# Attention in a fixed order: the four PSUM score banks as one tile, and as two tiles of one step each

## The chip, the core and the metric

The kernel runs on one NeuronCore of one Trainium2 chip, as one program. Its time is the device time of that core in microseconds, and the number that counts is the median of several executions. The inputs and the output lie in the chip's memory; the host only rearranges the inputs before the start.

## The reference

Three stages follow each other. The change is in the first.

```python
def _attn_ref(q, k, v):                      # (4, 8, 576, 64) each
    scores = scale * np.matmul(q, k.transpose(0, 1, 3, 2))
    rel = pos[:, None] - pos[None, :]
    bias = slopes[:, None, None] * (-np.abs(rel))[None]
    mask = (rel >= 0) & (rel < 128)
    scores = np.where(mask, scores + bias[None], -1e9)
    attn = np.exp(scores - scores.max(-1, keepdims=True))
    attn = attn / (attn.sum(-1, keepdims=True) + 1e-9)
    return np.matmul(attn, v)

def _moe_ref(x, phi, w1, w2):                # x: (2304, 512), 8 experts, 4 slots each
    logits = x @ phi
    d = softmax of logits over the tokens;  c = softmax over the slots
    slots = d.T @ x
    slot_out[e] = np.maximum(slots[e] @ w1[e], 0) @ w2[e]
    return c @ slot_out

def _moe2_ref(x, w_in, w_out):               # d_ff = 2048
    h = x @ w_in
    return (h * np.clip(h + 3, 0, 6) / 6) @ w_out
```

All data are 32-bit floats. A row of the scores has at most 128 valid keys, since the window is 128.

## The kernel before

**The steps.** There are four batches `b`. In a batch the 576 tokens are cut into five tiles `i` of 128 rows (the last has 64), and the eight heads into four couples `j`. One (b, i, j) is a step, 80 in all, and two steps that follow each other are a pair: 40 pairs, two for each tile. Below, pair "1a" is the first pair of a tile with i = 1, pair "1b" its second.

**One step.** `emit_s` (L179 to L212) does four small matmuls on TensorE (L190), one for each head (`u`) and half of the 64 rows (`hf`). Their output is `sp[64e..., m, hf, c0:c1]`, where `m` is the step's place in its pair (0 or 1) and `hf` picks the half. The tile `sp` (L148) is 128 x 2 x 2 x 512 floats, so that each (m, hf) fills a PSUM bank of its own: two banks for the first step of a pair, two for the second. VectorE then reads each half out of PSUM (L202): it scales it, adds the bias and keeps the smallest value of each row. ScalarE takes the exponent and the row sums (L210). After both steps of a pair VectorE makes the reciprocals (`emit_norm`, L217 and L219) and GpSimd multiplies (L224). Two steps later TensorE transposes the result (`emit_t`, L237) and VectorE or ScalarE copies it out (L239). Four steps later TensorE multiplies it with V (`emit_pv`, L257).

**Side work.** For every finished tile there are smaller steps: `side_x` (transposes L274, copy L277), `side_l` (L283, L285), and, for groups of tiles, `side_max` (L296, L298 to L321), `side_e` (L328, L335, L336) and `side_s` (L345, L351). Those that write PSUM share one buffer, the tag `m`.

**What sets the order.** It is written by hand. Inside `manual_schedule` (L477) each engine gets its instructions as the Python code issues them, in the sequence of L30 for each pair: `s0 s1 p0 p1 b0 t0 n0 t1 x0`, that is both steps' scores, two products with V of the pair before last, one piece of side work, two transposes with the norm between them, another piece of side work. No engine takes a later instruction ahead of an earlier one that waits. The semaphores are not written by hand: they follow from which tile an instruction writes and which it reads.

**Transfers.** SP's queue issues them in the order of `do_s` (L434): at the first pair of tile m, q of tile m+1, k and v of tile m+2 (256 KB each), then one expert weight (1 MB). From tile 17 on it issues weights until no buffer is free. A transfer whose buffer is still being read holds back all that stand behind it on that queue.

**Other users of the score banks.** `last_l` (L359) and `last_max` (L391) at the end of attention, and the matmuls at L506 that keep TensorE busy before the next stage, borrow parts of `sp`.

Of the kernel before, what the change touches and what calls it, by code (L numbers as in the profile page):

```python
# [9 lines left out]
F32 = mybir.dt.float32  # L10
# [34 lines left out]
def nq(i):  # L45
    return 128 if i < 4 else 64
# [3 lines left out]
def body(ctx: ExitStack, tc, q, k, v, phi, we, wf, cst, sel, out):  # L50
    nc = tc.nc
# [3 lines left out]
    ident, blk, dup = conp[:, 0:128], conp[:, 128:256], conp[:, 256:384]  # L55
# [73 lines left out]
    with ExitStack() as a:  # L129
# [9 lines left out]
        ps_s = a.enter_context(tc.tile_pool(name="ps_s", bufs=1, space=PSUM))  # L139
# [5 lines left out]
        bias8 = cona.rearrange("p (j h c) -> p j h c", j=NP, h=2)  # L145
        xb = [tp.tile([128, 2, 2, 128], F32, name=f"xb{n}") for n in range(2)]
        pb = [tp.tile([128, 448], F32, name=f"pb{n}") for n in range(NPB)]
        sp = ps_s.tile([128, 2, 2, 512], F32, name="sp")  # L148
        acc = cp.tile([128, 128], F32, name="acc")
        el = cp.tile([128, S], F32, name="el")  # L150
        vt = {}
# [27 lines left out]
        def emit_s(n):  # L179
            b, i, j = steps[n]  # L180
            hs = halves(i)
            w, m = nq(i), n % 2
            for e in range(2):
                for u in range(2):
                    hf = u ^ e
                    if hf >= len(hs):
                        continue
                    c0, c1 = hs[hf][1:]
                    g = 2 * (i - 1) + hf
                    nc.tensor.matmul(  # L190
                        out=sp[64 * e:64 * e + 64, m, hf, c0:c1],
                        lhsT=qz[64 * u:64 * u + 64, (NB * b + i) % 2,
                                j * w + 64 * hf:j * w + 64 * hf + 64],
                        rhs=kt[64 * u:64 * u + 64, g + c0 // 64:g + 3, j],
                        start=True, stop=True)
            p = pb[n % NPB]
            P[n] = p
            if not m:
                ST[0] = sm.tile([128, 3, 4], F32, tag="st", name=f"st{n}")
            st = ST[0]  # L200
            for hf, c0, c1 in hs:
                nc.vector.tensor_tensor_reduce(  # L202
                    out=p[:, 256 * hf + c0:256 * hf + c1],
                    in0=sp[:, m, hf, c0:c1], in1=bias8[:, j, hf, c0:c1],
                    scale=-0.125, scalar=3.0e38, op0=ALU.add, op1=ALU.min,
                    accum_out=st[:, 0, 2 * m + hf:2 * m + hf + 1])
            for hf, c0, c1 in hs:
                x = p[:, 256 * hf + c0:256 * hf + c1]
                r = slice(2 * m + hf, 2 * m + hf + 1)
                nc.scalar.activation(out=x, in_=x, func=AF.Exp, bias=st[:, 0, r], scale=-1.0,  # L210
                                     accum_out=st[:, 1, r])
            return p, st, hs  # L212
# [74 lines left out]
        run = {}  # L287
# [66 lines left out]
        def last_l(i):  # L354
            c0, w = 128 * (i - 3), nq(i)
            if i == 3:
                run["lg"] = sp[:, 0, 0, 0:192]
            for j in range(NP):
                nc.tensor.matmul(out=run["lg"][:, c0:c0 + w],  # L359
                                 lhsT=phi4[:, j].rearrange("p g s -> p (g s)"),  # L360
                                 rhs=xt[B - 1, i][:, j, 0:w], start=j == 0, stop=j == NP - 1)

        def last_max():
            mx = ep.tile([128, 8], F32, tag="mx", name="mxl")
            lg, nm, al, z, fz = run["lg"], mx[:, 2:3], mx[:, 6:7], mx[:, 4:5], mx[:, 5:6]
            nc.vector.reduce_max(out=mx[:, 0:1], in_=lg, axis=AX.X)
            nc.vector.scalar_tensor_tensor(out=nm, in0=mx[:, 0:1], scalar=-1.0, in1=run["nm"],
                                           op0=ALU.mult, op1=ALU.min)
            nc.scalar.copy(out=el[0:32, 0:192], in_=lg[0:32])
            nc.scalar.activation(out=el[:, 256:448], in_=lg, func=AF.Exp, bias=nm, accum_out=z)  # L370
            nc.scalar.activation(out=al, in_=run["nm"], func=AF.Exp, bias=nm, scale=-1.0)
            t = ps_m.tile([128, 2, 2, NS], F32, tag="m", name="lnl")
            for r in (1, 0):
                for i in range(2):
                    o = 256 * r + 128 * i
                    nc.tensor.transpose(out=t[0:nq(3 + i), i, r], in_=el[0:32, o:o + nq(3 + i)],
                                        identity=ident[0:32, 0:32])
            e = ep.tile([128, NB, NS], F32, tag="e", name="el2", bufs=1)
            nc.scalar.copy(out=e[:, 0], in_=t[:, 0, 1])
            nc.scalar.copy(out=e[0:64, 1], in_=t[0:64, 1, 1])  # L380
            nc.vector.scalar_tensor_tensor(out=z, in0=run["z"], scalar=al, in1=z,
                                           op0=ALU.mult, op1=ALU.add)
            nc.vector.tensor_scalar(out=fz, in0=z, scalar1=EPS, scalar2=None, op0=ALU.add)
            nc.vector.reciprocal(out=fz, in_=fz)
            nc.vector.tensor_scalar(out=acc, in0=acc, scalar1=al, scalar2=fz, op0=ALU.mult,
                                    op1=ALU.mult)
            t2 = sp[:, 0, 1, 0:128]
            for i in range(2):
                w = nq(3 + i)
                for g in range(4):  # L390
                    nc.tensor.matmul(out=t2[32 * g:32 * g + 32, :], lhsT=e[0:w, i],  # L391
                                     rhs=xn[B - 1, 3 + i][0:w, 128 * g:128 * g + 128],
                                     start=i == 0, stop=i == 1)
            nc.vector.scalar_tensor_tensor(out=acc, in0=t2, scalar=fz, in1=acc, op0=ALU.mult,
                                           op1=ALU.add)
            o = NB * (B - 1) + 3
            nc.scalar.copy(out=cn[:, o], in_=t[:, 0, 0])
            nc.scalar.copy(out=cn[0:64, o + 1], in_=t[0:64, 1, 0])
# [102 lines left out]
        for c in range(2):  # L501
            nc.vector.tensor_copy(
                out=sT2[:, 2 * c:2 * c + 2],
                in_=t[:, 2 * c:2 * c + 2].to_broadcast([128, 2, 2, NS]))
        for _ in range(WARM_A):
            nc.tensor.matmul(out=sp[:, 1, 0, 0:128], lhsT=ident, rhs=ident, start=True, stop=True)  # L506
    pools["z"] = xctx.enter_context(tc.tile_pool(name="zpool", bufs=1, side="left",
                                                 reuse_waits="tile"))
    free["z"] = 1
# [96 lines left out]
    with ExitStack() as bx:  # L606
# [4 lines left out]
        with tc.manual_schedule():  # L611
# [7 lines left out]
                                    in1=rm[:, 0].unsqueeze(2).to_broadcast(wide),  # L619
# [7 lines left out]
                                    in1=rm[:, 1].unsqueeze(2).to_broadcast(wide),  # L627
# [99 lines left out]
            for n in range(16):  # L727
                G, fc = n // 8, n % 8
                w = take(16 + n)
                for g in range(4):  # L730
                    nc.tensor.matmul(out=so[32 * g:32 * g + 8, :], lhsT=hz[:, fc, G, g, :],
                                     rhs=w[g], start=n == 0, stop=n == 15)
# [17 lines left out]
            for G in range(2):  # L750
                L["last"] = nc.vector.tensor_copy(
                    out=L["soT"][:, :, 16 * G:16 * G + 16].rearrange("p c (g j) -> p c g j", g=4),
# [308 lines left out]
```

## Time and profile before

| | us |
|---|---|
| three runs | 416.51, 417.2, 419.62 (median 417.2) |
| the profiled execution's own time | 420.83 |
| its span, first to last instruction | 419.0 |
| score matmuls L190: first and last start | 6.1, 201.0 |
| TensorE busy | 354.7 (85% of the span) |
| VectorE, ScalarE, GpSimd busy | 195.5, 184.7, 81.7 |
| mean granted TensorE clock, share of full speed | 0.918 |

The profile shows one execution. Busy shares are means over stages with quite different limits, so a wait has to be read in its stage: attention fills the span from about 6 to 212 us. On an engine with a fixed order a wait delays all that follows it on that engine. A matmul's end is modelled, so where two groups of matmuls follow each other the distance of their starts says more than their lengths. The granted clock is 1.00 or 0.50 in any short stretch, which is 2.4 or 1.2 GHz.

### The profile page before, as it was taken

To read this page: it belongs to the slowest core of one execution; us is meant where nothing else is said; L and a number is where in the kernel's file an instruction comes from. 1 tells how busy PE (TensorE), PEld (TensorE's weight loads), DVE (VectorE), ACT (ScalarE), POOL (GpSimd) and SP (SyncE) were. 2 spreads that over 40 slices of the span, in tenths; PEclk is the share of its full clock that TensorE was granted. 3 is DMA by queue.
4 is the path that set the end of the run, shared out by engine and by line. 5 is a ranking of instruction groups with operands and counts; after the bars stand their busy time and mean duration, and the time that the engine had idled before them with its cause. 6 is when DMAs were issued, how large, how long until landed. Compare 5 with 4: busy or idle time off the path is not lost. (4 is left out here: it accounts for less than half of the span.)

```text
span 419.0 us, 7556 instructions
## 1 busy us (share of the span) xinstructions
PE 354.7 (85%) x2738; PEld 211.1 (50%) x2738; DVE 195.5 (47%) x617; ACT 184.7 (44%) x551; POOL 81.7 (20%) x182
## 2 busy tenths in 40 slices
PE   6887877778778878786879995599999999999995
PEld 5455544454445544554553321343333436878883
DVE  1454445544354434453242108488888737871000
ACT  3566566656576665563421133522222205642210
POOL 2334223333234223331100220000000001210000
PEclk9599999989699995997959999569999999999999
DMA  8406574445714467091586999886200000112112
GB/s 276 128 21 217 196 261 163 153 175 177 302 40 152 178 230 274 13 360 70 200 296 251 424 383 418 364 276 225 101 0 2 1 1 19 59 75 77 75 75 82
DMA packets 19835, 71.10 MB, mean 170 GB/s; under 512 B 2672, under 2 KB 4848, under 8 KB 13776
## 3 DMA queue, kind: packets, MB, share of 16 engines
q1 hardware_dynamic: 18576, 69.08, 44.6%
q10 hardware_dynamic: 1216, 1.47, 1.0%
q8 instruction: 23, 0.38, 0.4%
q14 instruction: 20, 0.16, 0.1%
HBM read 65.83 MB, written 4.72 MB: 168 GB/s over the span
## 5 line engine op out<-in xcount | busy, mean ns | idle before, releaser
L224 POOL TENSOR_TENSOR pb<-pb,st 128x192 f32<-128x192 f32 (+2 forms) x144 | 63.3, 470 | 140.1 <-DVE st L219 65.4
L210 ACT ACTIVATE pb<-pb,st 128x192 f32<-128x192 f32 (+2 forms) x144 | 61.9, 430 | 46.0 <-DVE st L202 46.0
L190 PE MATMUL sp<-kt,qz 64*64 64x192 f32 (+2 forms) x576 | 46.9, 361 | 34.5 <-DVE st L202 32.5
L202 DVE CUSTOM_DVE_ANT_0 pb<-sp,cona 128x192 f32<-128x192 f32 (+2 forms) x144 | 43.3, 333 | 60.9 <-PE sp L190 50.8
L805 PE MATMUL q<-F,mf 128*128 128x512 f32 x128 | 63.3, 628 | 3.8 <-DVE mf L793 3.8
L190 PEld LDWEIGHTS sp<-kt,qz 64*64 64x64 f32 x576 | 17.7, 143 | 57.2 <-DVE st L202 47.3
L257 PE MATMUL o<-xb,v 128*64 128x128 f32 (+2 forms) x576 | 44.3, 289 | 0.1
L838 PE MATMUL acc<-qhi,P 128*128 128x512 f32 x140 | 42.1, 395 | 0.0
L237 PE MATMUL t<-conp,pb 128*128 128x128 f32 x256 | 41.4, 306 | 0.0
L805 PEld LDWEIGHTS q<-F,mf 128*128 128x128 f32 x128 | 23.3, 197 | 33.4 <-issue 22.6
L257 PEld LDWEIGHTS o<-xb,v 128*64 128x64 f32 (+1 forms) x576 | 32.8, 145 | 13.4 <-issue 11.3
L237 PEld LDWEIGHTS t<-conp,pb 128*128 128x128 f32 x256 | 32.1, 157 | 5.4 <-issue 3.3
L838 PEld LDWEIGHTS acc<-qhi,P 128*128 128x128 f32 x140 | 25.9, 188 | 6.1
L239 ACT COPY xb<-t 128x512 f32<-128x512 f32 (+1 forms) x40 | 19.7, 493 | 19.6 <-PE t L237 19.5
L239 DVE COPY xb<-t 128x512 f32<-128x512 f32 (+1 forms) x40 | 23.2, 580 | 10.8 <-PE t L237 10.2
L210 ACT ACTIVATION_READ_ACCUMULATOR pb<-pb,st 128x1 f32 x144 | 26.9, 187 | 0.0
L853 ACT ACTIVATE out<-acc 128x512 f32<-128x512 f32 (+1 forms) x18 | 10.5, 585 | 30.9 <-PE acc L838 23.3
L838 PE MATMUL acc<-qlo,P 128*128 128x512 f32 x56 | 22.1, 395 | 0.0
L795 POOL COPY mf<-mt 128x64 f32<-128x64 f32 x8 | 5.9, 735 | 80.2 <-ACT mt L785 53.7
L777 ACT COPY m<-mp 128x256 f32<-128x256 f32 x8 | 3.0, 372 | 42.0 <-PE mp L774 42.0
L274 PE MATMUL xps<-conp,xt 128*128 128x128 f32 (+1 forms) x76 | 13.1, 298 | 9.0 <-ACT el L314 8.5
L585 DVE TENSOR_TENSOR pf<-R,As 128x512 f32<-128x512 f32 (+1 forms) x20 | 12.7, 637 | 14.1 <-ACT As L569 7.8
(153 smaller groups left out, 454.6 us busy)
## 6 DMA issues: line engine op xcount, KB each, us to landing
w<-in_we_dram SPq DMA_DIRECT2D x30, 1024.0 KB, 6.3
w<-in_wf_dram SPq DMA_DIRECT2D x16, 1024.0 KB, 8.1
out_dram<-out SPq DMA_DIRECT2D x17, 256.0 KB, 2.0
v<-in_v_dram SPq DMA_DIRECT2D x16, 256.0 KB, 2.8
qz<-in_q_dram SPq DMA_DIRECT2D x15, 256.0 KB, 5.0
kt<-in_k_dram SPq DMA_DIRECT2D x15, 256.0 KB, 5.5
kt<-in_we_dram SPq DMA_DIRECT2D x1, 1024.0 KB, 7.3
qz<-in_q_dram SPq DMA_DIRECT2D x6, 128.0 KB, 5.2
```

The costliest lines, as they stand in the source:

```text
L190: nc.tensor.matmul(out=sp[64 * e:64 * e + 64, m, hf, c0:c1], lhsT=qz[64 * u:64 * u + 64, (NB * b + i) % 2, j * w + 64 * hf:j * w + 64 * hf ...
L202: nc.vector.tensor_tensor_reduce(out=p[:, 256 * hf + c0:256 * hf + c1], in0=sp[:, m, hf, c0:c1], in1=bias8[:, j, hf, c0:c1], scale=-0.125, ...
L210: nc.scalar.activation(out=x, in_=x, func=AF.Exp, bias=st[:, 0, r], scale=-1.0, accum_out=st[:, 1, r])
L224: nc.gpsimd.tensor_tensor(out=x, in0=x, in1=st[:, 2, 2 * m + hf:2 * m + hf + 1].to_broadcast([128, c1 - c0]), op=ALU.mult)
L237: nc.tensor.transpose(out=t[:, c, hf], in_=p[:, o:o + 128], identity=ident)
L239: f(out=x[:, p0:2, 0:nh], in_=t[:, p0:2, 0:nh])
L257: nc.tensor.matmul(out=o[64 * u:64 * u + 64, j, 0:w], lhsT=vv[0:kk, 128 * j + 64 * u:128 * j + 64 * u + 64], rhs=y, start=m == 0, stop=m = ...
L274: nc.tensor.transpose(out=t[0:w, j, :], in_=xt[b, i][:, j, 0:w], identity=ident)
L585: nc.vector.tensor_tensor(out=pf, in0=t[:, 0:w], in1=(L["a2"][s % 2] if j == 4 else A[s])[:, 0:w], op=ALU.mult)
L805: nc.tensor.matmul(out=Q[pt], lhsT=mm[p][:, u, 128 * pt:128 * pt + 128], rhs=F[:, u], start=p == u == 0, stop=p == 7 and u == 1)
L838: nc.tensor.matmul(out=acc, lhsT=l, rhs=r[:, j], start=j == 0 and i == 0, stop=j == 4 and i == 1)
L853: nc.scalar.activation(out=o[:, cs], in_=acc[:, cs], func=AF.Copy, scale=1.0 / 6.0))
```

## The change

The one tile `sp` of four banks becomes a list of two tiles with two banks each, `sp[0]` for the first step of a pair and `sp[1]` for the second. Shapes, sizes and the number of banks in use stay as they were.

```diff
-        sp = ps_s.tile([128, 2, 2, 512], F32, name="sp")
+        sp = [ps_s.tile([128, 2, 512], F32, name=f"sp{n}") for n in range(2)]
...
-                        out=sp[64 * e:64 * e + 64, m, hf, c0:c1],
+                        out=sp[m][64 * e:64 * e + 64, hf, c0:c1],
...
-                    in0=sp[:, m, hf, c0:c1], in1=bias8[:, j, hf, c0:c1],
+                    in0=sp[m][:, hf, c0:c1], in1=bias8[:, j, hf, c0:c1],
...
-                run["lg"] = sp[:, 0, 0, 0:192]
+                run["lg"] = sp[0][:, 0, 0:192]
...
-            t2 = sp[:, 0, 1, 0:128]
+            t2 = sp[1][:, 1, 0:128]
...
-            nc.tensor.matmul(out=sp[:, 1, 0, 0:128], lhsT=ident, rhs=ident, start=True, stop=True)
+            nc.tensor.matmul(out=sp[1][:, 0, 0:128], lhsT=ident, rhs=ident, start=True, stop=True)
```

No engine gets an instruction more, fewer or in another place. What differs is which event an instruction waits for. On TensorE, the first pair of the program (pair 0a of the first batch, L190), before; the name in brackets is the semaphore, here VectorE's:

```order
L190 MATMUL sp<-kt,qz 64x64 [waits DMAHW2_49,DMAHW1_49]
L190 MATMUL sp<-kt,qz 64x128 x2
L190 MATMUL sp<-kt,qz 64x64
L190 MATMUL sp<-kt,qz 64x64 [waits DVE_49]
L190 MATMUL sp<-kt,qz 64x128 x2
L190 MATMUL sp<-kt,qz 64x64
```

and with the change, where 116 and 117 are the two new tiles:

```order
L190 MATMUL sp_116<-kt,qz 64x64 [waits DMAHW2_49,DMAHW1_49]
L190 MATMUL sp_116<-kt,qz 64x128 x2
L190 MATMUL sp_116<-kt,qz 64x64
L190 MATMUL sp_117<-kt,qz 64x64
L190 MATMUL sp_117<-kt,qz 64x128 x2
L190 MATMUL sp_117<-kt,qz 64x64
```

The second step's matmuls had waited for VectorE's two readings (L202) of the first step, which lie in other banks; that wait is gone. In later pairs both programs show a wait on VectorE at both steps, but for other readings. The second pair of the second tile on TensorE, before:

```order
L190 MATMUL sp<-kt,qz 64x192 [waits DVE_49]
L190 MATMUL sp<-kt,qz 64x192 x3
L190 MATMUL sp<-kt,qz 64x192 [waits DVE_49]
L190 MATMUL sp<-kt,qz 64x192 x3
L257 MATMUL o_0_233<-xb_110,v_0_140 64x128 x2
```

and the same pair with the change:

```order
L190 MATMUL sp_116<-kt,qz 64x192 [waits DVE_49]
L190 MATMUL sp_116<-kt,qz 64x192 x3
L190 MATMUL sp_117<-kt,qz 64x192 [waits DVE_49]
L190 MATMUL sp_117<-kt,qz 64x192 x3
L257 MATMUL o_0_234<-xb_110,v_0_141 64x128 [waits DVE_49]
L257 MATMUL o_0_234<-xb_110,v_0_141 64x128
```

Each step now waits for the readings of the step in the same place of the pair before; in the program before, the second step waited for those of the first step of its own pair. The product with V (L257) shows a wait for VectorE's copy L239 of the pair before, which the earlier wait at L190 used to include. There are 60 such places at L190, 38 at L257 and one at L359; VectorE, ScalarE, GpSimd and SP wait for what they waited for.

## Rows read from the trace of the kernel before

**Rows 1.** The page: span, and busy time of the first two engines and the others

```profile
span 419.0 us, 7556 instructions
...
PE 354.7 (85%) x2738; PEld 211.1 (50%) x2738; DVE 195.5 (47%) x617; ACT 184.7 (44%) x551; POOL 81.7 (20%) x182
```

**Rows 2.** Waits of PE up to 204 us: total us, times, longest

```profile
PE sp L190 <- DVE st L202: 32.5, 41, 1.1
```

**Rows 3.** Timeline of PE, pairs 3b and 4a: start, length, instruction, idle before

```profile
133.73 0.56 PE L190 MATMUL sp<-kt,qz 64*64 64x192 f32 x8
135.16 0.56 PE L190 MATMUL sp<-kt,qz 64*64 64x192 f32 x8 [0.88 <-DVE st L202]
135.65 1.09 PE L257 MATMUL o<-xb,v 128*64 128x128 f32 x16
...
139.72 0.54 PE L190 MATMUL sp<-kt,qz 64*64 64x192 f32 x4
140.84 0.54 PE L190 MATMUL sp<-kt,qz 64*64 64x192 f32 x4 [0.58 <-DVE st L202]
141.31 1.09 PE L257 MATMUL o<-xb,v 128*64 128x128 f32 x16
```

**Rows 4.** Timeline of PE, pair 0b

```profile
53.85 0.44 PE L190 MATMUL sp<-kt,qz 64*64 64x64 f32 x8
54.97 0.44 PE L190 MATMUL sp<-kt,qz 64*64 64x64 f32 x8 [0.67 <-DVE st L202]
55.34 1.12 PE L257 MATMUL o<-xb,v 128*64 128x64 f32 x16
```

**Rows 5.** Timeline of all engines, pairs 1a and 1b

```profile
60.99 0.44 ACT L210 ACTIVATE pb<-pb,st 128x192 f32<-128x192 f32 x1
...
61.97 0.46 ACT L210 ACTIVATE pb<-pb,st 128x192 f32<-128x192 f32 x1 [0.45 <-DVE st L202]
...
62.87 0.19 ACT L335 COPY e<-ln 128x64 f32<-128x64 f32 x1
...
63.09 0.22 DVE L336 COPY cn<-ln 128x64 f32<-128x64 f32 x1 [0.87 <-ACT e L335]
...
63.37 0.32 PE L283 MATMUL lps<-xt,phi 128*32 128x64 f32 x8 [0.53 <-DVE cn L336]
...
67.07 0.56 ACT L268 COPY xt<-o 128x512 f32<-128x512 f32 x1
...
67.69 0.66 PE L274 MATMUL xps<-conp,xt 128*128 128x128 f32 x4
```

**Rows 6.** Timeline of SP's queue, tiles 17 and 18

```profile
178.18 2.35 SPq L114 DMA_DIRECT2D w<-in_we_dram  x4
180.57 0.44 SPq L161 DMA_DIRECT2D qz<-in_q_dram  x1
```

**Rows 7.** Timeline of PE, pair 4a of the last batch

```profile
192.53 0.54 PE L190 MATMUL sp<-kt,qz 64*64 64x192 f32 x4 [2.01 <-issue]
```

**Rows 8.** Windows, whole pairs: stretch, us, busy time of engines, clock, DMA share, GB/s

```profile
59.41:68.27 8.86, 6.58 (x91) 4.08 (x90) 5.00 (x27) 5.96 (x22) 3.16 (x8) 1.00 0.89 340
108.45:118.99 10.54, 8.79 (x92) 5.11 (x91) 4.89 (x26) 6.08 (x22) 3.15 (x8) 0.70 0.68 261
157.40:169.71 12.31, 10.34 (x91) 6.62 (x90) 5.34 (x27) 6.16 (x22) 3.37 (x9) 0.58 0.62 234
139.72:143.98 4.26, 3.68 (x44) 2.45 (x43) 2.31 (x10) 2.11 (x8) 1.90 (x4) 1.00 0.75 298
89.01:94.83 5.82, 5.24 (x44) 3.73 (x43) 2.55 (x11) 2.11 (x8) 1.90 (x4) 0.71 0.46 184
```

**Rows 9.** Windows just before the clock fell to 0.50, same columns

```profile
87.50:90.90 3.40, 1.93 (x19) 1.11 (x20) 1.51 (x7) 2.63 (x8) 1.02 (x3) 1.00 1.01 393
104.60:108.00 3.40, 2.08 (x21) 1.54 (x20) 0.98 (x7) 2.37 (x10) 0.00 (x0) 1.00 0.60 177
155.80:159.20 3.40, 1.48 (x20) 0.78 (x20) 1.45 (x8) 2.62 (x9) 1.17 (x4) 1.00 1.02 390
```

## The prediction

> **What bounds the kernel now.** I read the page's busy times first: TensorE is busy 354.7 of 419.0 us, every other engine less than half [rows 1]. A share of 85% is a mean over stages, so next come the waits of TensorE in attention alone. One line stands out: its score matmuls (L190) wait 41 times, 32.5 us in all, for VectorE's reading L202 [rows 2]. The timeline of one pair shows where. The first step's matmuls start at 133.73, the second step's at 135.16 after an idle 0.88 us, and the product with V follows at 135.65 [rows 3]. The second group takes 0.49 us from its start to the next group's, so the first could have handed over after as long, and did so after 1.43. The order of the two programs says why: the second step waited for readings of the first, although it writes other banks. TensorE is what sets attention's pace, and this is the largest hole in it.
>
> **What the change takes out.** With two tiles the second step waits for the readings of the pair before, which were done long ago. TensorE gets to the product with V earlier by the excess of the first distance over the second:
> - tiles 1 to 3: 1.43 - 0.49 = 0.94, call it 0.95 us [rows 3], in 24 pairs;
> - tile 4: (140.84 - 139.72) - (141.31 - 140.84) = 1.12 - 0.47 = 0.65 us [rows 3], in 8 pairs;
> - tile 0: (54.97 - 53.85) - (55.34 - 54.97) = 1.12 - 0.37 = 0.75 us [rows 4], in 8 pairs.
>
> That is 22.8 + 5.2 + 6.0 = 34.0 us, near the 32.5 of the waits. No instruction is added or moved on any engine. The wait that L257 now carries (VectorE's copy of the transposes of the pair before) ends about where a pair begins, and the product comes two groups of score matmuls later: nothing.
>
> **What is late next.** The gap was also time for others. VectorE's first reading of a pair does not move, and so ScalarE's first exponent does not either, counted from the pair's start. What moves is the second step: in pair 1a ScalarE now starts the second step's first exponent at 61.97, having waited 0.45 us [rows 5]. Without the gap it starts when its own previous one is through, 60.99 + 0.44 = 61.43. ScalarE gains 0.54 us where TensorE gains 0.95. Pairs in which TensorE's last side step hangs on work that stands behind the exponents on ScalarE gain 0.54 only:
> - 1a: L335 at 62.87, then VectorE's L336 at 63.09, then TensorE's L283 at 63.37 after an idle 0.53 us [rows 5]; it just waits longer;
> - 1b: the copy L268 runs from 67.07 for 0.56 us, and L274, which needs it, starts at 67.69 [rows 5]: there TensorE waits for nothing yet, but would;
> - 2b: the same two chains at once.
>
> In 2a, 3a and 3b, and in tiles 0 and 4, either nothing on ScalarE is waited for at the end, or the chain starts from TensorE's own earlier step (the maxima of `side_max`) and moves with it. So a batch gains 3 x 0.95 + 3 x 0.54 + 2 x 0.75 + 2 x 0.65 = 7.27 us, and four batches 29.1.
>
> Two corrections. The first pair has no other work to hide behind: its normalisation must be through before the first transposes, and ScalarE's order lets it come a little earlier only; I take 0.6 us off. And the last batch waits for a transfer. Four weights are issued at 178.18, the q of the last tile behind them at 180.57 [rows 6], and TensorE waits 2.01 us for it at 192.53 [rows 7]. The pairs between (2b, 3a, 3b) would bring TensorE there 0.54 + 0.95 + 0.95 = 2.44 us earlier, but the issue waits for the product with V in 2b and comes only 0.95 earlier; 4 MB in between take as long as before. 1.5 us are given back. **At an unchanged clock** the gain is 29.1 - 0.6 - 1.5 = 27.0 us.
>
> All that follows attention is released by its end (weights are fetched into buffers that it frees), so it moves as a whole.
>
> **The clock.** In attention the granted clock fell to 1.2 GHz at 90.9, 108.0 and 159.2 us. I price a fall by whole pairs: tile 1 takes 8.86 us at full clock, 10.54 and 12.31 with a fall; pair 4a 4.26 and 5.82 [rows 8]. That is 1.7 + 3.5 + 1.6 = 6.8 us. Ahead of the falls TensorE had been busy 1.93, 2.08 and 1.48 of 3.4 us [rows 9], 44 to 61%, where tile 1 at full clock has 6.58 of 8.86, 74% [rows 8]. The first of these stretches contains the gap of pair 4a and the third that of pair 1a; without it they would be busy 1.93/2.75 = 70% and 1.48/2.45 = 60%. The second has its idle time from `side_max`, which stays. I count the first fall as gone and the other two as half gone: 1.6 + 2.6 = 4.2, and 0.3 for the start, where the clock is low too and the same gaps close: 4.5 us. The bounds are 0 and 6.8.
>
> The Trainium skill ("TensorE: Matmul & The Clock Gate", section "Why this matters for your kernels") puts a fall in the middle of a kernel down to one long idle gap between bursts of matmuls. The only gap of 2 us in these stretches is the transfer's [rows 7]. By that rule these score gaps are not what lowers the clock, and the sum would stay at the 27.0 us; the rows show falls without a long gap, after stretches that were idle in pieces, so I go by them and keep the rule's case as a rival.
>
> **Sum.** 420.83 (the profiled execution's own time) - 27.0 - 4.5 = 389.3; I say **389.5**. That execution lies 3.6 us above the median of the runs, 417.2, so against the median the change is worth 27.7 us or 6.6%.
>
> **The rivals.**
> - The clock does not care: what lowers it is not these gaps, and the falls stay as many and as long. 420.8 - 27.0 = 393.8, or 392 to 397 with some chains tighter than I think. This is what the skill's rule amounts to. For it: pair 0b has much idle in every batch and the clock fell after two of them only. Chance 0.18.
> - ScalarE holds every pair. If 0.54 were the most that any pair of tiles 1 to 3 gains, and 0.4 the most in the others, it is 24 x 0.54 + 16 x 0.4 - 2.1 = 17.3 us, and with up to 3 us of clock 400 to 404. Against it: pair 3a has no side step on ScalarE before its end. Chance 0.07.
> - All of it comes out: 34.0 and 6.8, so 380. For it: a slower clock makes TensorE slower and leaves the others more slack. Chance 0.10 for 378 to 385.
> - The gap turns up elsewhere in full (GpSimd's products late for the transposes, say), no change: 414 to 421. The order of the programs speaks against the change not doing what it says; the wait at the first pair is gone. Chance 0.02.
> - Slower: the transfers become the bound. SP's queue has 3 x 256 KB and 1 MB for a tile, about 1.8 MB, and at 393 GB/s [rows 9] that takes 4.6 us. Tile 1 now has 8.86 us [rows 8] and would have 7.8. If q came late all the same, each time would cost what the one such wait cost: 2.01 us [rows 7], and a fall of the clock after it of about 1.6. With 27 us gained, it takes 8 late tiles of 16 to lose it all; 12 would give 420.8 - 27 + 12 x 3.6 = 437. Against it: one such wait only, behind four weights at once. Chance 0.02.
>
> My forecast (386 to 392) has the remaining 0.61. With it, the clock's rival and the upper half of "all of it" the range is 382 to 398, which leaves out 380 and less and all from ScalarE's case on. One per cent, 4.2 us, is about what a measurement of this kernel can tell from no change: faster by more 0.96, within it 0.02, slower 0.02.
>
> **What the profile after would show.** The line L190 <- L202 in TensorE's waits gone or below 2 us; the two score groups of a full pair 0.5 us apart; L202 no longer than before, since it has always read while other banks were written; in 1a, 1b and 2b new or longer waits before L283 and L274, about 0.4 us each, none of weight in 2a and 3a; the wait for q in the last batch grown to about 3.5 us; the last score matmuls near 171 us rather than 201; fewer stretches at 0.50 between 23 and 165 us; everything behind attention as long as it was. I would be wrong if the transposes (L237) waited for GpSimd, if q were late in earlier tiles, or if the later stages, which I only shift, met their weights late.

## The result, and the profile after

The changed kernel takes **377.7 us** (median of 3 runs, 376.4 to 379.3) where the kernel before took 417.2: a ratio of 0.904, interval 0.896 to 0.912. The forecast was 389.5 with a range of 382 to 398: the direction is right, the gain is 39.5 us instead of 27.7, and the time lies below the range. The profiled execution took 379.32 us; against that of before, 420.83, it is 41.5 us less. Ratios leave out executions that took over 1.5% more than the fastest of their kernel, and the profiled one of the kernel before, at a mean clock of 0.918, was such a one.

The page's first lines, to be read beside [rows 1]: the span is 41.6 us shorter with the same 2738 matmuls, and TensorE's busy time is 18.5 us shorter too.

```profile
span 377.4 us, 7557 instructions
...
PE 336.2 (89%) x2738; PEld 205.7 (55%) x2738; DVE 192.3 (51%) x617; ACT 178.7 (47%) x551; POOL 82.3 (22%) x182
```

Which part became shorter is seen with the span cut at the last group of score matmuls, at 199.26 us before and 159.07 after (windows: stretch, its length, busy us of PE, PEld, DVE, ACT and POOL with their instructions, granted clock, DMA share, GB/s). Before:

```profile
0.00:199.26 199.26, 154.67 (x1741) 102.40 (x1742) 87.09 (x451) 120.20 (x425) 62.76 (x150) 0.90 0.50 178
199.26:419.00 219.74, 199.99 (x1001) 108.74 (x997) 108.39 (x166) 64.52 (x127) 18.97 (x33) 0.93 0.43 162
```

After:

```profile
0.00:159.07 159.07, 135.35 (x1742) 96.81 (x1742) 83.68 (x450) 114.22 (x425) 62.78 (x149) 0.99 0.61 223
159.07:377.40 218.33, 200.87 (x1001) 108.89 (x997) 108.62 (x169) 64.46 (x127) 19.50 (x33) 0.94 0.43 163
```

Attention is 40.2 us shorter, the rest 1.4. In attention TensorE's idle time fell from 44.6 to 23.7 us, and its busy time from 154.7 to 135.4 for the same matmuls, at a mean clock of 0.99 instead of 0.90. But not all of the 19.3 us of busy time is the clock's. Over the whole span 13.3 of it is L190's own, by the page (before, then after):

```profile
L190 PE MATMUL sp<-kt,qz 64*64 64x192 f32 (+2 forms) x576 | 46.9, 361 | 34.5 <-DVE st L202 32.5
L190 PE MATMUL sp<-kt,qz 64*64 64x192 f32 (+2 forms) x576 | 33.6, 318 | 4.9 <-issue 3.6
```

The ends of matmuls are modelled, and two groups that stand apart count 0.56 us each [rows 3], where the two together count 0.88 (below): 0.24 us less in a full pair, an estimated 9 us over the 40 pairs. So about 9 of the 19.3 belong to the gap and about 10 to the clock.

TensorE's waits up to 165 us (total us, times, longest). The line L190 <- L202 of [rows 2] is gone. What leads now waits for ScalarE and VectorE. The first line was there before the change too (7.5 us up to 204 us); the waits for L336 and L268, 1.0 us in all before, are now 6.6:

```profile
PE xps L274 <- ACT el L314: 7.9, 7, 1.3
PE sp L190 <- issue: 3.6, 1, 3.6
PE lps L283 <- DVE cn L336: 3.2, 3, 1.1
...
PE xps L274 <- ACT xt L268: 2.3, 5, 0.6
...
PE xps L274 <- DVE cn L336: 1.1, 3, 0.4
```

The timeline of PE (start, length, instruction, idle before) in pairs 1a and 2b of later batches. In the profile each of the program's four matmuls of a step counts as two. The two groups of score matmuls are now one row, x16, with no idle time inside; before they were two rows with 0.88 us between [rows 3]:

```profile
46.41 0.63 PE L274 MATMUL xps<-conp,xt 128*64 128x128 f32 x4 [1.32 <-ACT el L314]
46.97 0.88 PE L190 MATMUL sp<-kt,qz 64*64 64x192 f32 x16
47.78 0.66 PE L257 MATMUL o<-xb,v 128*64 128x128 f32 x8
48.37 0.34 PE L328 MATMUL ln<-conp,el 64*128 64x64 f32 x2
48.63 0.66 PE L237 MATMUL t<-conp,pb 128*128 128x128 f32 x4
50.37 0.32 PE L283 MATMUL lps<-xt,phi 128*32 128x64 f32 x8 [1.08 <-DVE cn L336]
...
97.93 0.88 PE L190 MATMUL sp<-kt,qz 64*64 64x192 f32 x16
98.74 1.09 PE L257 MATMUL o<-xb,v 128*64 128x128 f32 x16
```

From the first group to the product with V it is 0.81 us (46.97 to 47.78), where it was 1.92 [rows 3]. In pair 1a TensorE waits 1.08 us before L283, where it waited 0.53 [rows 5]: about half of what it saved is lost there again.

The wait for q in the last batch, on SP's queue and on TensorE, beside [rows 6, 7]:

```profile
139.58 2.24 SPq L114 DMA_DIRECT2D w<-in_we_dram  x4
141.86 0.45 SPq L161 DMA_DIRECT2D qz<-in_q_dram  x1
```

```profile
154.09 1.08 PE L190 MATMUL sp<-kt,qz 64*64 64x192 f32 x8 [3.61 <-issue]
```

And the clock, in windows of the kernel after: full from 4.4 us to the end of that wait, where before it was at 0.50 in four stretches up to there, 34 us in all (9.0 to 22.6, and the three falls of [rows 8, 9]). In attention it falls once, right after the 3.61 us:

```profile
4.40:154.60 150.20, 127.53 (x1692) 90.30 (x1692) 81.86 (x441) 112.72 (x419) 61.61 (x140) 1.00 0.63 231
154.60:158.00 3.40, 3.40 (x26) 2.46 (x23) 0.95 (x5) 1.30 (x5) 0.00 (x0) 0.50 0.02 5
```

**The account.** Attention's 40.2 us by the starts of pairs: up to pair 2a of the first batch 5.2 (22.38 to 17.22); from there to the last batch's 4a 33.3 (170.15 to 136.87); that pair 1.75. Comparing pairs of one kind that ran at full clock in both traces gives what the gap alone was worth: 1.02 to 1.11 us in 2a, 3a and 3b; 0.54 to 0.56 in 1a, 1b and 2b; 0.89 to 0.90 in 0a and 0b; 0.60 in 4a (0.80 in the first batch) and 0.80 in 4b. That is about 27.8 over the middle stretch, less 1.6 for the longer wait for q; so about 7.0 of the 33.3 are the clock's.

### The profile page after: what moved, and what is told of

The parts are those of the page before. It is cut to its first block, busy times and chain, and to the rows that moved or that the text cites. A ratio compares the mean times of both kernels' runs of the same rounds, so it can differ in the third digit from the quotient of the medians.

```text
span 377.4 us, 7557 instructions
## 1 busy us (share of the span) xinstructions
PE 336.2 (89%) x2738; PEld 205.7 (55%) x2738; DVE 192.3 (51%) x617; ACT 178.7 (47%) x551; POOL 82.3 (22%) x182
## 5 line engine op out<-in xcount | busy, mean ns | idle before, releaser
L202 DVE CUSTOM_DVE_ANT_0 pb<-sp,cona 128x192 f32<-128x192 f32 (+2 forms) x144 | 40.6, 332 | 28.3 <-PE sp L190 25.8
L257 PE MATMUL o<-xb,v 128*64 128x128 f32 (+2 forms) x576 | 41.5, 276 | 0.1
L237 PE MATMUL t<-conp,pb 128*128 128x128 f32 x256 | 39.3, 284 | 2.0 <-POOL pb L224 1.2
L190 PE MATMUL sp<-kt,qz 64*64 64x192 f32 (+2 forms) x576 | 33.6, 318 | 4.9 <-issue 3.6
L257 PEld LDWEIGHTS o<-xb,v 128*64 128x64 f32 (+1 forms) x576 | 30.8, 138 | 12.4 <-issue 7.9
L237 PEld LDWEIGHTS t<-conp,pb 128*128 128x128 f32 x256 | 28.6, 143 | 9.5 <-POOL pb L224 5.8
L239 DVE COPY xb<-t 128x512 f32<-128x512 f32 (+1 forms) x40 | 23.2, 580 | 6.9 <-PE t L237 6.5
L190 PEld LDWEIGHTS sp<-kt,qz 64*64 64x64 f32 x576 | 19.6, 132 | 12.7 <-issue 8.0
L853 ACT ACTIVATE out<-acc 128x512 f32<-128x512 f32 (+1 forms) x18 | 10.6, 586 | 30.9 <-PE acc L838 23.3
L239 ACT COPY xb<-t 128x512 f32<-128x512 f32 (+1 forms) x40 | 19.7, 492 | 7.8 <-PE t L237 7.6
L274 PE MATMUL xps<-conp,xt 128*128 128x128 f32 (+1 forms) x76 | 12.3, 284 | 12.3 <-ACT el L314 8.9
L585 DVE TENSOR_TENSOR pf<-R,As 128x512 f32<-128x512 f32 (+1 forms) x20 | 12.7, 637 | 14.1 <-ACT As L569 7.8
```

Of the source, the lines that this page charges most:

```text
L190: nc.tensor.matmul(out=sp[m][64 * e:64 * e + 64, hf, c0:c1], lhsT=qz[64 * u:64 * u + 64, (NB * b + i) % 2, j * w + 64 * hf:j * w + 64 * hf ...
L202: nc.vector.tensor_tensor_reduce(out=p[:, 256 * hf + c0:256 * hf + c1], in0=sp[m][:, hf, c0:c1], in1=bias8[:, j, hf, c0:c1], scale=-0.125, ...
L237: nc.tensor.transpose(out=t[:, c, hf], in_=p[:, o:o + 128], identity=ident)
L239: f(out=x[:, p0:2, 0:nh], in_=t[:, p0:2, 0:nh])
L257: nc.tensor.matmul(out=o[64 * u:64 * u + 64, j, 0:w], lhsT=vv[0:kk, 128 * j + 64 * u:128 * j + 64 * u + 64], rhs=y, start=m == 0, stop=m = ...
L274: nc.tensor.transpose(out=t[0:w, j, :], in_=xt[b, i][:, j, 0:w], identity=ident)
```

## The experiments

The theory: the gap cost its idle time and, through idle time in pieces, the clock. The rivals: the clock does not depend on these gaps; or something other than the wait (the number of tiles) made the difference. All results below are medians, with the ratio to the kernel before run beside them on the same chip (417.6, 417.3 and 416.1 us in the three sets). "Last scores" is when the last group of score matmuls starts in the profiled execution, "low" how long the clock was at 0.50 up to there; both are of one execution. Mean clocks differ between executions of one program: 39 executions of the kernel before had 0.914 to 0.949, with a median of 0.929.

| run | us | ratio, interval | last scores | low |
|---|---|---|---|---|
| before | 417.2 | | 199.3 | 40 |
| after | 377.7 | 0.904, 0.896-0.912 | 159.1 | 3.4 |
| tie_all | 424.2 | 1.017, 1.007-1.027 | 208.9 | 58 |
| tie_fill | 422.1 | 1.011, 1.007-1.016 | 202.1 | 17 |
| tie_fit | 412.4 | 0.993, 0.988-0.998 | 192.3 | 3.4 |
| tie_start | 381.0 | 0.919, 0.911-0.926 | 163.2 | 14 |
| tie_idle | 395.4 | 0.949, 0.941-0.957 | 179.5 | 37 |
| tie_dense | 396.6 | 0.953, 0.946-0.961 | 176.9 | 17 |
| split_hf | 416.5 | 1.003, 0.998-1.007 | 194.5 | 24 |
| four | 374.2 | 0.897, 0.889-0.906 | 159.8 | 6.8 |
| late_w | 374.7 | 0.902, 0.895-0.909 | 154.4 | 0 |
| best | 364.3 | 0.876, 0.868-0.885 | 147.9 | 3.4 |
| best2 | 363.9 | 0.871, 0.862-0.879 | 147.5 | 6.8 |

What follows the last scores took 212 to 220 us in all these executions, with no order to it (211.9 in `four`, 218.3 in the kernel after, which has the same code there); its own clock falls differ from one execution to the next. So small differences are read from attention, not from the medians. The low stretch of `best` and `best2` lies at the start (from 10.6 and 9.8 us), that of `four` around the wait for q.

**The wait put back.** Ahead of the second step's matmuls, one matmul of a single column goes to an unused column of the first step's tile. It must wait for VectorE's readings of that tile, and the second step, behind it on TensorE, waits with it:

```diff
             w, m = nq(i), n % 2
+            if m:
+                hf = hs[-1][0]
+                g, r = 2 * (i - 1) + hf, slice(64 * hf, 64 * hf + 64)
+                nc.tensor.matmul(out=sp[0][0:64, hf, 448:449],
+                                 lhsT=qz[r, (NB * b + i) % 2, j * w:j * w + 64],
+                                 rhs=kt[r, g + 2, j, 0:1], start=True, stop=True)
```

> The two tiles stay, but in every pair a matmul of one column writes an unused column of the first step's tile just ahead of the second step's matmuls, so that TensorE waits again for VectorE's readings of the first step. If that wait is all that the change took out: about 417 us (412 to 423), the two score groups 1.4 us apart, and the clock back at 0.50 in places between 9 and 165 us. If something else about two tiles made the kernel faster (another placement, the other waits that moved): well below 400.

424.2 us, just above the first range, which had no room for the ties' own time. The wait of 0.88 us is back in its place, now before the tie (L186):

```profile
87.99 0.56 PE L196 MATMUL sp<-kt,qz 64*64 64x192 f32 x8
89.42 0.21 PE L186 MATMUL sp<-kt,qz 64*64 64x1 f32 x1 [0.88 <-DVE st L208]
...
90.00 0.77 PE L263 MATMUL o<-xb,v 128*64 128x128 f32 x10
```

From group to product it is 2.01 us against 1.92 before; the tie costs 0.1 in each of 40 pairs, 4 us. The falls of the clock are back, in this execution more of them than before the change; it was the longest of its four (427.6 us at a mean clock of 0.906, the others 420.7 to 426.3 at 0.914 to 0.937). So the wait alone undoes the whole gain.

**The wait back, the idle time filled.** The same tie, and before it matmuls that nobody reads, so that TensorE waits busy:

```diff
+        def fill(n, hs):
+            for _ in range(0 if n < 4 else len(hs) + 2 if steps[n][1] else 3):
+                nc.tensor.matmul(out=sp[1][:, 0, 256:384], lhsT=ident, rhs=ident, start=True,
+                                 stop=True)
...
+                fill(n, hs)
```

> As the run with the wait in every pair, but the gap is filled with three or four 128x128 matmuls of constants into unused columns of the second tile; TensorE waits as long and does no more useful work, but is not idle. Theory (the clock depends on how idle TensorE is in a stretch, and the change got about 11 us from it): the clock stays at 1.00 in attention, as it does with the change, and the time is 8 to 14 us below the run with the bare wait, 402 to 410. Rival (the falls have nothing to do with these gaps and the change met a better moment): the falls come as before and the time is that of the run with the bare wait or a few us more, 415 to 424.

422.1 us: a miss, and by the time alone the rival's forecast. The fillers took longer than the gap: the two groups stood 1.58 us apart instead of 1.44 in full pairs, 1.35 instead of 1.13 in tile 4, some 6 us in all. The clock did mostly as the theory says: 17 us low instead of 58, of these 6.9 at the start, where the first two pairs had no fillers, and 6.8 around the wait for q. The next run has fewer fillers, from the first pair on:

```diff
-            for _ in range(0 if n < 4 else len(hs) + 2 if steps[n][1] else 3):
+            for _ in range(3 if steps[n][1] % 4 else 2):
```

> The wait is back in every pair, and the gap is filled with matmuls whose result nobody reads, three in pairs of tiles 1 to 3 and two in tiles 0 and 4, from the first pair on: fewer than in the run before with fillers, so that the second step starts no later than the wait lets it (distance of the two score groups 1.44, 1.13 and 1.12 us as with ties alone). If idle time in pieces is what lowers the clock, the granted clock stays at 1.00 in attention up to the wait for q, pairs have their length at full clock (a batch 48.2 us, where ties alone gave 52.7 and 53.1), and the time is 410 to 416. If the clock does not care for these gaps, or only for useful work, the falls stay and the time is that of ties alone, 421 to 427.

412.4 us, as expected, and by the ratios (0.993 and 1.017) about 10 us below ties alone. Its ten executions took 410.0 to 416.2 us at mean clocks of 0.953 to 0.969, all below the four with ties alone in time and above them in clock. The windows are three batches, each from its first pair on (the last to its pair 4a); ties alone first, then with fillers:

```profile
50.24:102.94 52.70, 42.06 (x485) 27.63 (x484) 22.81 (x118) 31.36 (x112) 15.83 (x36) 0.87 0.46 168
102.94:156.06 53.12, 42.48 (x485) 28.31 (x484) 22.78 (x117) 31.37 (x112) 15.84 (x36) 0.87 0.46 167
156.06:201.88 45.82, 34.32 (x390) 22.40 (x390) 19.31 (x101) 27.29 (x99) 13.98 (x33) 0.85 0.56 212
```

```profile
48.27:98.00 49.73, 46.20 (x536) 32.13 (x535) 22.73 (x118) 31.28 (x112) 15.84 (x36) 0.97 0.50 179
98.00:146.31 48.31, 44.77 (x537) 31.21 (x536) 22.68 (x117) 31.27 (x112) 15.84 (x36) 1.00 0.51 184
146.31:187.91 41.60, 35.97 (x435) 25.01 (x434) 19.20 (x101) 27.20 (x99) 14.06 (x33) 1.00 0.60 232
```

TensorE does more work, waits for the same readings at the same places, and is 3 to 5 us faster in each batch. Pairs that ran at full clock in both are equally long (2a 5.07 us, 3b 6.08); the difference lies in the pairs at the low clock. So idle time in gaps of 0.6 to 0.9 us is what tipped the clock, and matmuls in them prevented all falls but one short one (in the first of these batches). With the ties' 4 us added, the kernel before lies 199.3 + 4.0 - 192.3 = 11.0 us above this run in attention, and by the medians 417.3 + 4.0 - 412.4 = 8.9: the worth of the clock there, found a second way.

**Only the first four pairs tied** (`if m and n < 8`).

> The wait for the readings of the first step is put back in the first four pairs only (tiles 0 and 1 of the first batch), by a one-column matmul into an unused column of the first score tile. The question is what part of the gain at the start was the clock's. If the gaps of these pairs also held the clock down at the start, 1.20 GHz returns for about 8 us between 9 and 23 us, the first score matmuls of pair 2a of the first batch start near 21.8 (17.2 without the tie, 22.4 before the change), and the time is 381 to 384. If the clock at the start has nothing to do with them, only the fixed part returns, about 0.5 us in each of four pairs: 2a starts near 19.3 and the time is 379 to 380.5. Later pairs are as in the changed kernel in either case.

381.0 us. Pair 2a started at 21.64, and the clock was low again from 11.2 to 21.4:

```profile
11.30:21.60 10.30, 8.69 (x60) 5.86 (x60) 4.48 (x24) 5.26 (x19) 3.38 (x9) 0.51 0.35 113
```

The last scores start at 163.2, 4.1 us later than in the kernel after, so the gaps bring the low clock at the start back too; in tie_fit, with the same four ties but filled, it was full there and 2a started at 19.78. Not the gaps alone can do it: `best` and `best2` (below), without any tie, were low at the start for 3.4 and 6.8 us, behind a wait of 1.42 us at the first transposes. The median rises by 3.3 only, to the lower end of the first range.

**Which gaps lower the clock.** Tied pairs of two kinds, 16 in each run: those around the stretches that wait most (3b, 4a, 0b, 1a), and those that are dense (1b, 2a, 2b, 3a).

```diff
+            if m and (i, n // 2 % 2) in ((3, 1), (4, 0), (0, 1), (1, 0)):   # tie_idle
+            if m and (i, n // 2 % 2) in ((1, 1), (2, 0), (2, 1), (3, 0)):   # tie_dense
```

> The wait is back in 16 pairs only, those around the maxima of side_max that were the most idle (3b, 4a, 0b, 1a). By the pair lengths of the two traces at full clock it costs 4 x (1.0 + 0.7 + 0.9 + 0.55) = 12.6 us: 390 without a fall of the clock. Theory: these are the pairs ahead of which and in which the clock fell, so falls come back between 23 and 155 us, and the time is 393 to 398. Rival (any gaps do, or none): 390, the same as the other 16 pairs.

395.4 us, as expected, with one fall in each batch at 0b or 1a (in the first batch from 11.7 us), as in these windows of the other three:

```profile
52.70:62.90 10.20, 9.33 (x85) 5.41 (x84) 4.49 (x25) 5.66 (x22) 3.15 (x8) 0.50 0.77 293
100.40:107.30 6.90, 6.90 (x68) 4.48 (x65) 3.13 (x17) 4.16 (x18) 1.90 (x4) 0.51 0.80 299
144.80:151.60 6.80, 6.80 (x68) 4.38 (x65) 3.09 (x17) 4.07 (x18) 1.90 (x4) 0.50 0.78 292
```

> The wait is back in 16 pairs only, the denser ones (1b, 2a, 2b, 3a). By the pair lengths it costs 4 x (0.55 + 1.04 + 0.56 + 1.10) = 13.0 us. Theory (the clock falls where TensorE is idle for much of a stretch): no fall in attention, 389 to 392. Rival (every gap counts alike for the clock): falls as in the other run with 16 pairs, 394 to 398.

396.6 us: a miss, and the time that the rival gave, by which every gap counts alike. The clock was low less long than in tie_idle, 17 us against 37, but it fell in three of four batches as well, in 1b, right behind 0b and 1a (in the first batch from 15.1 us):

```profile
56.10:62.90 6.80, 6.31 (x54) 4.55 (x54) 2.37 (x12) 3.37 (x11) 2.34 (x6) 0.50 0.57 208
144.80:151.60 6.80, 6.23 (x51) 4.54 (x54) 2.38 (x12) 3.30 (x11) 2.13 (x5) 0.50 0.39 143
```

So the division was too simple: a gap need not lie in a pair that waits much. That it adjoins one may be enough, but this is not shown; in the third batch the same program had no fall.

**Two tiles, shared out the other way**: one for each `hf`, that is for each half of the tile's rows, used by both steps. (The expectation calls `hf` a half of the heads; by the code the heads are `u`.)

```diff
-                        out=sp[m][64 * e:64 * e + 64, hf, c0:c1],
+                        out=sp[hf][64 * e:64 * e + 64, m, c0:c1],
...
-                    in0=sp[m][:, hf, c0:c1], in1=bias8[:, j, hf, c0:c1],
+                    in0=sp[hf][:, m, c0:c1], in1=bias8[:, j, hf, c0:c1],
```

> The changed kernel with the same two tiles of two banks each, but shared out the other way: a tile for each half of the heads (hf), which both steps of a pair use, in place of a tile for each step. If what counts is which matmuls share a tile with which readings, the second step waits again: for the first reading instead of the last one of the first step, so its first matmul starts 1.1 to 1.2 us after the first step's (1.43 before the change), its second one at 1.4; tile 4, with one half only, has 1.12 as before. The clock falls return in part. The time is 411 to 418. If the number of tiles is what counts, it is near 378.

416.5 us, no different from before. The second group starts 1.15 us after the first, 0.28 (one reading) earlier than before, but its next matmuls wait for the second reading, so that it takes 0.76 instead of 0.49 and the product starts after 1.91 instead of 1.92:

```profile
81.75 0.56 PE L190 MATMUL sp<-kt,qz 64*64 64x192 f32 x8
82.90 0.83 PE L190 MATMUL sp<-kt,qz 64*64 64x192 f32 x8 [0.60 <-DVE st L202]
83.66 0.77 PE L257 MATMUL o<-xb,v 128*64 128x128 f32 x10
```

The number of tiles is not what counts; what counts is which writes share one with which readings. Where the clock was full in both, the pairs are as long as before the change to 0.02 us. Yet this execution had one of the three falls of [rows 8, 9] only, the last, and its last scores start 4.8 us earlier: with the gaps in place, too, falls can stay away.

**Four tiles of one bank.**

```diff
-        sp = [ps_s.tile([128, 2, 512], F32, name=f"sp{n}") for n in range(2)]
+        sp = [[ps_s.tile([128, 512], F32, name=f"sp{n}_{h}") for h in range(2)] for n in range(2)]
...
```

> The changed kernel with four tiles of one bank each. If the change has taken out the whole of the wait, nothing is left for a finer division: score groups 0.38 us apart and 376 to 379. If the readings of one half still hold the other half's matmuls or the other way round, VectorE's first reading starts up to 0.1 us earlier in a pair and up to 4 us are gained: 373 to 375.

374.2 us, in the second range by its median, but for another reason: pairs are as long as in the kernel after, and the last scores start 0.7 us later. The difference lies behind attention, in the part with the same code (211.9 against 218.3 us). Nothing is left of the wait for a finer division to remove.

**The weights behind the last q.**

```diff
-                    while load_next_w() and m > 16:
+                    while load_next_w() and m > 17:
```

> The changed kernel with the four weight transfers that stand ahead of the last q issued one tile later, behind it (one of them stays where it was). If the 3.6 us wait for q at 154 us is only the queue's order, it goes, with the fall of the clock behind it (1.2 us in the pair after): 372 to 374. If the weights are what the stage behind attention waits for, the 3 to 5 us come back there, between 165 and 230 us, and the time stays at 376 to 378.

374.7 us, just above the first range. SP's queue now has q ahead of three of the weights, and TensorE starts pair 4a without waiting for it:

```profile
139.93 0.59 SPq L114 DMA_DIRECT2D w<-in_we_dram  x1
140.57 0.43 SPq L161 DMA_DIRECT2D qz<-in_q_dram  x1
141.04 1.83 SPq L114 DMA_DIRECT2D w<-in_we_dram  x3
```

```profile
150.17 0.66 PE L274 MATMUL xps<-conp,xt 128*128 128x128 f32 x4 [0.97 <-ACT el L314]
150.76 0.87 PE L190 MATMUL sp<-kt,qz 64*64 64x192 f32 x8
```

Attention ends 4.7 us earlier, without a fall of the clock, and the rest is no longer for it (216.9 us). The 3.6 us were the queue's order. By the medians the gain is within the noise: the intervals of the two ratios overlap.

**Two copies from ScalarE to VectorE**, L268 and L335, which stood behind the exponents, on top of the later weights.

```diff
-                nc.scalar.copy(out=xt[b, i][:, :, 0:w], in_=o[:, :, 0:w])
+                nc.vector.tensor_copy(out=xt[b, i][:, :, 0:w], in_=o[:, :, 0:w])
...
-                    nc.scalar.copy(out=e[0:w, a0:a1], in_=t[0:w, a0:a1, 1])
+                    nc.vector.tensor_copy(out=e[0:w, a0:a1], in_=t[0:w, a0:a1, 1])
```

> The kernel with the later weights, and with two copies moved from ScalarE, where they stand behind the exponents, to VectorE: the output of attention (one for a tile) and the transposed weights of the landmarks. If ScalarE's queue is what holds pairs 1a, 1b and 2b to a gain of 0.55 us, TensorE's waits for these copies (about 0.4 us each, 11 to 15 of them) go and the time is 4 to 6 us below the kernel with later weights alone: 367 to 370. If the copies delay VectorE's own chain (copies of transposes, normalisation) by as much as they free ScalarE, nothing is gained or up to 3 us is lost: 372 to 377.

364.3 us, below the first range: 10 below late_w by the medians, of which 6.5 lie in attention (154.4 to 147.9). That is what TensorE's waits for these copies came to in the kernel after (3.2 + 2.3 + 1.1); where the rest comes from is not shown. In pair 1a L283 follows the transposes with no idle time, and the pair takes 2.59 us instead of 3.65:

```profile
48.64 0.66 PE L237 MATMUL t<-conp,pb 128*128 128x128 f32 x4
49.32 0.32 PE L283 MATMUL lps<-xt,phi 128*32 128x64 f32 x8
49.57 0.72 PE L190 MATMUL sp<-kt,qz 64*64 64x192 f32 x12
```

This is the version that beats both kernels. One wait is left on top of its list:

```profile
PE xps L274 <- ACT el L314: 8.5, 8, 1.3
```

**The maxima's logits in the second score tile**, on top of `best`.

```diff
-                t = ps_m.tile([128, 512], F32, tag="m", name=f"lt{b}_{c0}")
+                t = sp[1][:, 1, 192:512]
```

> The fastest version so far (later weights, two copies on VectorE) with the logits of the side step of the maxima (lt) put into unused columns of the second score tile, in place of the one bank that all side steps share. TensorE waits there 11 times, 9.8 us in all, for ScalarE's reading L314 of lt before its next side step may write that bank. If these waits only come from the shared bank they go, and the time is 7 to 10 us lower than 364.3: 354 to 357. But lt now stands in a tile with the second step's scores, so the next pair's second step waits for the same reading, some 0.9 us later in the program than the side step did: if ScalarE is that late, a part of the wait comes back there, and the time is 358 to 362.

363.9 us: nothing gained, and by neither way foreseen. The wait is gone, and TensorE hardly waits for L314's reading at the second step either (`L190 <- ACT el L315` in the first fence below). It waits one step later instead, at the product with V:

```profile
PE o L257 <- DVE xb L239: 4.4, 10, 1.3
...
PE sp L190 <- ACT el L315: 0.8, 2, 0.4
```

```profile
93.83 0.22 DVE L322 SCALAR_TENSOR_TENSOR mx<-mx,mx 128x1 f32<-128x1 f32 x1 [0.98 <-ACT mx L317]
93.97 0.69 DVE L239 COPY xb<-t 128x512 f32<-128x512 f32 x1
```

VectorE waits 0.98 us for ScalarE's last operation of the maxima before it copies the transposes that the product needs. Pair 0b became 1.5 us shorter and 1a 1.4 longer (1.2 and 1.0 in the third batch), 3b 0.9 shorter and 4a 1.1 longer: nearly all of it given back in the next pair.

## Why the prediction was right in kind and wrong in size

By the terms of its sum, for attention up to the last scores, where it comes to 30.9 us (without the last pair's 0.65) and 40.2 were measured:

- **The wait goes, and nothing takes its place on VectorE or GpSimd: right** but for the start, where the transposes (L237) wait for GpSimd twice, 1.2 us in all. The line of [rows 2] is gone, L202 takes 332 ns as before (333), and split_hf and four show that it was the sharing of a tile.
- **The direct term was too small: 2.6 us.** I took 0.49 us from the second group as what a group needs [rows 3]. That group had just waited. Back to back the first hands over after 0.38 and the two need 0.81, so a full pair saves 1.11, not 0.95; tile 0 0.90 instead of 0.75, tile 4 0.79 instead of 0.65 by the same distances (4a got 0.60 of it in three batches).
- **ScalarE holds 1a, 1b and 2b: right**, 0.54 to 0.56 for a forecast of 0.54; the wait before L283 grew by 0.55 us, and best showed these waits to be ScalarE's queue.
- **The wait for q: right**, 3.61 for a forecast of 3.5; late_w showed it to be the order on the queue.
- **The clock is the step that failed**: 4.5 forecast, about 11 measured between the two profiled executions, 9 by the medians of tie_fit and the kernel before.
  - The three falls of [rows 8, 9]: I priced them at 6.8 and counted one as gone and two as half gone, 4.2. All three went, 7.0. I looked at each fall by itself and asked whether the gap closest to it tipped it; but each stretch lost several gaps, and tie_all and tie_fit show that together they decide. What I took for the cause of the second fall, the idle time of `side_max`, is unchanged: TensorE still waits 1.32 us there (the row at 46.41 above), and without the score gaps the clock stays full. How many falls an execution has is in part luck: split_hf had one of the three with all its gaps in place, and the one profiled before ran at a lower clock than most.
  - The start: I gave it 0.3 "where the clock is low too", with no price. By the prediction's own fixed terms the first four pairs gain 2.0; 5.2 came out, and tie_start gave 4.4 of them back with four ties, whose own time is about 0.4. It was the longest low stretch of attention, 13.6 us, and its windows stood open to be read as those of [rows 8] were. Before and after, up to pair 2a:

```profile
4.40:22.38 17.98, 14.10 (x111) 8.98 (x109) 7.28 (x44) 10.25 (x37) 4.86 (x13) 0.63 0.62 201
```

```profile
4.40:17.22 12.82, 9.68 (x111) 6.05 (x110) 6.94 (x44) 9.68 (x37) 4.95 (x14) 1.00 0.85 282
```

  - The same 111 matmuls were busy 14.1 us and now 9.7. The last batch's pair 4a, which I held fixed, gave another 1.1.
- **What follows moves as a whole: right** (219.7 and 218.3 us), but its clock varies by some us from run to run, so that medians move by that much.

The misses add up: 2.6 + 2.8 + 2.9 + 1.1 = 9.4, against 40.2 - 30.9 = 9.3. Of the 11.8 us between forecast and median, the other 2.5 are no step of the argument: what follows attention came out 0.7 shorter than the sum has it, the profiled execution lies 1.6 above the median of its kernel, and the sum was rounded up by 0.2. Starting it from the execution at 420.83, and not from the median of 417.2, had put the forecast 3.6 us higher from the outset. All misses of the steps have the same sign, and the case in which all comes out was put at 378 to 385 with a chance of 0.10; 377.7 is just below even that. It deserved more, since the clock's price was bounded from above by falls that I had chosen to look at.

The rival by which the clock does not care (393.8 us) has fallen with tie_fit and tie_idle. With it the rule in that section of the Trainium skill ("TensorE: Matmul & The Clock Gate", section "Why this matters for your kernels"), that one long gap is what brings the clock down, does not cover this case: here pieces of 0.6 to 1.3 us did. It does agree with the one fall in attention after the change, behind the 3.61 us. The transfer's 2.01 us of [rows 7], which the prediction set against that rule, come after all three falls of [rows 9]; the longest idle piece ahead of the last two was 1.32 us (L274). ScalarE did not hold every pair, and no transfer but that one came late.

## What to carry to other kernels

In this kernel waits between engines go by tile: two matmul groups that write different banks of one PSUM tile waited for each other's readers, so give each stage of a pipeline a tile of its own, and look at which reads share it, not at how many tiles there are. When a gap on TensorE repeats in every step, price the clock over every low stretch of the region, the start among them, and let the forecast's range reach to all of it being returned. Before taking out the next wait, look one step on: best2's was given back in the following pair, while best's was worth all of it because the work moved to an engine with more time to spare in attention (VectorE busy 83.7 of 159.1 us, ScalarE 114.2).

## What the runs showed of the hardware

- TensorE's granted clock depended on idle time in short pieces: with gaps of 0.6 to 0.9 us in each pair it was low for 24 to 58 us of attention (split_hf, before, tie_all), with the same gaps filled by useless matmuls for 3.4 (tie_fit), with none for 0 to 6.8 (after, four, late_w, best, best2).
- Matmuls that nobody reads made the kernel about 10 us faster than the same kernel without them (tie_fit and tie_all, ratios 0.993 and 1.017).
- A group of 8 matmuls that follows another directly costs less than one that starts after a wait: from start to the next group's start 0.81 us for two together (after), 0.49 for the one that had waited (before, [rows 3]).
